# Attention, MLP and spectral mixing on one core: channel products of two row blocks side by side, the first theta phase keyed sooner, one threshold per couple of rows, new costs in the build's order

## The chip, the cores and the metric

The kernel runs on one core of a Trainium2 chip. The metric is the device time in microseconds, the median of three runs. TensorE (PE) multiplies; VectorE (DVE), ScalarE (ACT) and GpSimd (POOL) work on tiles; SyncE (SP) issues most DMAs. PE accumulates in eight PSUM banks.

## The reference

Four batches of 576 tokens, 512 wide (8 heads of 64). Three stages follow each other:

```python
scores = scale * np.matmul(q, k.transpose(0, 1, 3, 2))
thresh = np.max(scores, axis=-1, keepdims=True) - tau
scores = np.where(scores >= thresh, scores, -1000000000.0)
attn = np.exp(scores - max); attn = attn / (sum + 1e-09); x = attn @ v

xn = (x - mu) / np.sqrt(var + 1e-06) * g_ln
x = x + np.maximum(xn @ w_ch1, 0.0) @ w_ch2          # 512 -> 2048 -> 512

theta = x @ w_theta                                   # 512 -> 512
y = w_tok_r @ (x * cos(theta)) + w_tok_i @ (x * sin(theta))   # over tokens
u = x + y
out = u + np.maximum(u @ w_ch, 0.0)                   # 512 -> 512
```

(The second and third blocks are shortened to their formulas.)

## The kernel before, in words

**The order of the work.** The program writes no order by hand. Each piece of work is an `op` with the engines that may do it and a cost in ns on each, the ops it depends on, the buffers that it takes and gives back (`Slot` of a `Res`), a kind and, for PE, a key. `Plan.run` (L124) places them one by one as a list scheduler: on PE, among the ops that can start at the same moment, the one with the lowest key goes first; on the other engines the one with the lowest ready time plus the kind's offset (`OFF`, L71). An op with several possible engines goes where it ends first by its costs. Instructions are issued on each engine in this order, so a changed cost can change engine and place of anything behind it. Where PE would stand idle for over 200 ns, `keep` (L339) puts small filler matmuls (`warm`, L345); this ends with attention.

**Precision.** fp32 products are made of fp32r parts: an operand is split into a high part (`hi`) and a rest (`lo`), and three matmuls replace one.

**Attention** takes batch by batch in couples of two row tiles (`couple`, L691; `unit` for each row). `qk` (L720) gives S; `top` (L784, DVE) reads S, writes E = -S and the row's extreme `bt`; `thresh` (L791 on ACT, L793 elsewhere) adds tau to a 128x1 tile, `thr`; `mask` (L797) and the exponential (L800) follow on ACT; then E is split and turned by DMA, and `pv` (L748) multiplies by v. The first half of the MLP (eight chunks of the hidden width, part A: first product `p_A` L515, hidden part `h_A`, second product `chA` L538) runs between, one group of three row tiles at a time. `ln_group` (L885) makes a group's normalised rows: norm on ACT (L935), three transposes on PE (`ptr`, L944), then a copy out of PSUM (`flat`) and the `hi` and `lo` parts.

**PSUM.** Four banks (`rM`) serve all through, four belong to S in attention. `turn` (L1049) gives those four to the group `rC`.

**Part B** does the other eight hidden chunks (steps of 12 `p_B` and 9 `c` matmuls) for the six groups (1,2), (1,0), (1,1), (0,0), (0,1), (0,2), the first number being the pair of batches. `cvt` (L350) makes weights' two parts from the raw ones in eight ops (DVE L375 to L392, POOL, ACT): `tok` for the token mix, `cw` for the channel product.

**Spectral stage**, one batch b at a time: `transposes(b)` (`pt`, L1241) and `thetas(b)` (`th`, `th_t`, L1288; five tiles), `make_z(b)` (x cos, x sin and their parts: `z`), `mix(b)` (`y`, L1451: 54 matmuls for each of four blocks of 128 channels; sums `u` L1473 and L1478 take the two banks of a block and give them back; then `x1T` and `x1Tl`, the parts of u), `chan(b)` (`o`, L1508: 24 matmuls for each block, 6 for each of the four blocks of u that it sums over; `uo`, L1521 and L1526). The first phase's key is set by `T0STEP` (L67), in steps of the last group of part B. Each block of `chan` took two banks of `rM`, and `ylast[1]` made each block's first product depend on the block before:

```python
sl = [Slot(rM), Slot(rM)]
...
o = op(mm(kk), [o or ylast[1], d["c"][kk], cw_ops[kk]], sl if kk == 0 else (), T=6 * mm_(288),
       key=key + 0.01 * c)
```

## Time and profile before

| | before |
|---|---|
| median of 3 runs | 943.57 us (943.29 to 943.91) |
| the profiled execution's own time | 943.46 us |
| its span (first to last instruction) | 941.6 us |
| mean granted clock of PE, 1 being full speed | 0.978 |
| PE, DVE, ACT, POOL busy | 888.4, 677.7, 530.2, 537.7 us |
| DMA | 111.93 MB, 119 GB/s on the mean |

Everything that is said of durations comes from this one profiled execution. Busy times are sums over instructions on an engine; for PE they hold the pipelined ends of matmuls, so a busy PE need not be a PE at its peak. A wait is idle time of an engine ahead of an instruction, with the instruction that ended it.

### The profile page before, as it was taken

Reading aid. Unit: us, or ns where it says so; the run is one execution under the profiler, and the core shown is the slowest. Engines: PE = TensorE matmul, PEld = TensorE weight load, DVE = VectorE, ACT = ScalarE, POOL = GpSimd, SP = SyncE. Lnnn points to the kernel's source line nnn. Section 1 sums busy time; section 2 is a strip of 40 time slices with the busy share of each in tenths; the row PEclk is TensorE's granted clock in tenths of the full one; section 3 lists DMA queues with packets and bytes.
Section 4 is the critical chain, followed back from the end, with each engine's and each line's share of the span. In section 5 each row is a group of like instructions: output and inputs, shape, how many; then the busy total and the mean of one; then the engine's idle time right before and its main releaser. Section 6 shows DMA issues by size and latency. Waiting matters only on the chain. (4 is left out here: it accounts for less than half of the span.)

```text
span 941.6 us, 18946 instructions
## 1 busy us (share of the span) xinstructions
PE 888.4 (94%) x7287; PEld 789.3 (84%) x7287; DVE 677.7 (72%) x1227; ACT 530.2 (56%) x968; POOL 537.7 (57%) x614
## 2 busy tenths in 40 slices
PE   9787879999999999999999999999989899999998
PEld 7665668878888888888888899989977789899998
DVE  6899989788897887783788692221489873697734
ACT  7787778888887878883556561111356330453300
POOL 5999899779887887781556771000266530263400
PEclk9898899999999999999999999999999899999999
DMA  7889796799789988792555660340021111010011
GB/s 195 171 189 184 168 199 119 138 227 176 148 180 174 184 183 145 158 165 48 190 168 168 202 190 7 100 154 1 1 77 57 28 42 39 12 63 1 14 38 51
DMA packets 224954, 111.93 MB, mean 119 GB/s; under 512 B 174048, under 2 KB 206304, under 8 KB 224864
## 3 DMA queue, kind: packets, MB, share of 16 engines
q1 hardware_dynamic: 224576, 110.72, 51.6%
...
q10 hardware_dynamic: 288, 0.00, 0.0%
...
## 5 line engine op out<-in xcount | busy, mean ns | idle before, releaser
L229 POOL TENSOR_TENSOR P<-E,P 128x64 f16<-128x64 f32 (+1 forms) x194 | 144.4, 759 | 14.6 <-DVE P L224 5.8
L784 DVE TENSOR_SCALAR_CACHE_REDUCE E<-S 128x576 f32<-128x576 f32 x144 | 105.4, 747 | 25.6 <-PE S L720 16.3
L797 ACT ACTIVATE E<-E,thr 128x576 f32<-128x576 f32 x144 | 108.0, 768 | 11.5 <-POOL thr L793 10.1
L515 PE MATMUL p_A<-xt,w 128*128 128x384 f32 x576 | 112.9, 343 | 1.7 <-issue 1.5
L1451 PE MATMUL y<-tok,z 128*128 128x288 f32 x768 | 109.7, 301 | 4.9 <-DVE u L1473 3.7
L515 PE MATMUL p_B<-xt,w 128*128 128x384 f32 x576 | 111.1, 341 | 1.4 <-DVE w L414 1.4
L538 PE MATMUL c<-w,h_B 128*128 128x512 f32 x432 | 108.9, 395 | 3.6 <-DVE h_B L524 2.0
L538 PE MATMUL chA<-w,h_A 128*128 128x512 f32 x432 | 111.0, 400 | 1.4 <-DVE h_A L524 1.4
L1451 PEld LDWEIGHTS y<-tok,z 128*128 128x128 f32 x768 | 106.2, 193 | 5.9 <-DVE u L1473 4.2
L515 PEld LDWEIGHTS p_B<-xt,w 128*128 128x128 f32 x576 | 103.8, 190 | 6.3 <-DVE w L414 2.3
L800 ACT ACTIVATE E<-E,ntaup 128x576 f32<-128x576 f32 x144 | 107.5, 767 | 0.9
L720 PE MATMUL S<-khi,q 64*128 64x288 f32 (+1 forms) x576 | 85.9, 328 | 21.3 <-DVE E L784 18.3
L515 PEld LDWEIGHTS p_A<-xt,w 128*128 128x128 f32 x576 | 98.2, 188 | 5.6 <-issue 4.3
L538 PEld LDWEIGHTS c<-w,h_B 128*128 128x128 f32 x432 | 80.1, 188 | 19.5 <-DVE h_B L524 3.1
L538 PEld LDWEIGHTS chA<-w,h_A 128*128 128x128 f32 x432 | 78.0, 188 | 18.2 <-issue 2.1
L748 PEld LDWEIGHTS <-PT 128*128 128x128 f16 (+1 forms) x2240 | 75.9, 101 | 17.0 <-issue 14.5
L720 PEld LDWEIGHTS S<-khi,q 64*128 64x128 f32 (+1 forms) x576 | 56.8, 192 | 37.6 <-DVE E L784 23.1
L748 PE MATMUL pv<-va,PT 128*128 128x65 f16 (+1 forms) x2240 | 84.1, 195 | 3.4 <-DVE va L224 2.3
L521 ACT ACTIVATE h_B<-p_B 128x384 fp32r<-128x384 f32 x48 | 23.6, 491 | 110.8 <-PE p_B L515 110.8
L524 DVE SCALAR_TENSOR_TENSOR h_B<-p_B,h_B 128x384 fp32r<-128x384 f32 x48 | 26.6, 553 | 72.6 <-ACT h_B L521 72.3
L229 DVE TENSOR_TENSOR P<-E,P 128x512 f16<-128x512 f32 (+1 forms) x94 | 69.6, 759 | 4.9 <-POOL P L226 3.3
L226 POOL TENSOR_SCALAR P<-E 128x576 f16<-128x576 f32 x85 | 64.7, 764 | 14.3 <-ACT E L800 13.0
...
## 6 DMA issues: line engine op xcount, KB each, us to landing
...
```

Of the source, the lines that this page charges most:

```text
L226: G.tensor_scalar(out=out, in0=in_, scalar1=1.0, scalar2=0.0, op0=ALU.mult, op1=ALU.add)
L229: e.tensor_tensor(out=out, in0=a, in1=b, op=ALU.subtract)
L515: T.matmul(st["ps"][:, :n], lhsT=ch.w1(a, c), rhs=xt()[:, c, bb, :n], start=(kk == 0), stop=(kk == 11))
L521: A.activation(out=st["h"][:, 0, :n], in_=st["ps"][:, :n], func=AF.Relu)
L524: V.scalar_tensor_tensor(out=st["h"][:, 1, :n], in0=st["ps"][:, :n], scalar=0.0, in1=f(st["h"][:, 0, :n]), op0=ALU.max, op1=ALU.subtract)
L538: T.matmul(ps, lhsT=h[:, a, t * 128:(t + 1) * 128], rhs=ch.w2(bb), start=(first and (a, bb) == M2[0]), stop=(stop and (a, bb) == M2[2]))
L720: T.matmul(w["S"][:, n, 0:288], lhsT=qd.q["t"][r, a, hp], rhs=d.k[bb][r, n * 288:(n + 1) * 288], start=(k == 0), stop=(k == 2))
L748: T.matmul(out[:, j * 65:j * 65 + n], lhsT=l, rhs=r[:, j * 65:j * 65 + n], start=(k == 0), stop=(k == len(seq) - 1))
L784: V.tensor_scalar(out=st["e"].rearrange("p (a k) -> p a k", a=2), in0=st["S"][:, :, 0:288], scalar1=-1.0, scalar2=None, op0=ALU.mult, op1= ...
L797: A.activation(out=st["e"], in_=st["e"], func=AF.Prelu, bias=st["thr"], scale=-1.0, alpha=STEEP)
L800: A.activation(out=st["e"], in_=st["e"], func=AF.Exp, bias=ntaup, scale=1.0)
L1451: T.matmul(st["ps"][n][:, 0:288], lhsT=a, rhs=w[:, n * 288:(n + 1) * 288], start=(k == 0 and q == 0), stop=(k == 8 and q == 2))
```

## The change

- `T0STEP` is 1 instead of 5: PE's keys for the first transposes and thetas stand four steps sooner in the last group of part B.
- Many costs are others: `gc` (two-input operations on POOL) 2.5 instead of 2.11 ns a column, DVE operations with two inputs from SBUF 1.5 instead of 1.04 (`V2`), single-input copies 0.95 instead of 0.52, the conversion steps 1.1, 0.95 and 1.45, `top` 830 instead of 880 ns.
- The conversion of `w_ch` gets a kind of its own, `late`, whose offset in `OFF` is 25000 instead of 6000.
- The two rows of a couple share `bt` and `thr` (128x2), and one `thresh` follows both tops; the masks read their column of it. `taup2` holds tau twice.
- `chan`: every other block takes its two banks from `rC`, and the dependence of a block on the block before is gone.
- Code for an unused way of turning E is removed.

The diff, cut; left out are `taup2`'s setup, the entry in `OFF`, and further costs that change in the same way:

```diff
@@ -64,11 +64,14 @@
-T0STEP = 5
+T0STEP = 1
...
+LATE = 25000.0
+GC = 2.5
+V2 = 1.5
...
@@ -244,7 +247,7 @@
-        return 145.0 + 2.11 * n
+        return 145.0 + GC * n
@@ -418,9 +422,9 @@
         ob = op(s1b, [o], A=ac(n), **kw)
-        o = op(s2a, [oa], G=gc1(n), V=vc(n, .52), **kw)
-        o = op(s2b, [o], V=vc(n, .52), **kw)
-        o = op(s2c, [o], (), [sa], V=vc(n), **kw)
+        o = op(s2a, [oa], G=1550.0, V=vc(n, 1.1), **kw)
+        o = op(s2b, [o], V=vc(n, .95), **kw)
+        o = op(s2c, [o], (), [sa], V=vc(n, 1.45), **kw)
         o = op(s3, [o, ob], G=gc(n), **kw)
@@ -772,29 +776,34 @@
             scaled(tile_)
 
-    def unit(st, o_qk, d, whole, pen0, kw, cp, spv, sx_):
+    def unit(st, us, o_qk, d, whole, pen0, kw, cp, spv, sx_):
 
         nm, j = st["nm"], st["j"]
...
         def top(e):
 
-            st["bt"] = ap.tile([128, 1], F32, tag="bt", bufs=8, name="bt_" + nm)
+            if "bt" not in cp:
+                cp["bt"] = ap.tile([128, 2], F32, tag="bt", bufs=6, name="bt_" + nm)
+            st["bt"] = cp["bt"][:, j:j + 1]
             st["e"] = ap.tile([128, 576], F32, tag=str(es), name="E_" + nm)
             V.tensor_scalar(out=st["e"].rearrange("p (a k) -> p a k", a=2), in0=st["S"][:, :, 0:288], scalar1=-1.0,
...
         def thresh(e):
 
-            st["thr"] = ap.tile([128, 1], F32, tag="thr", bufs=8, name="thr_" + nm)
-            if e is A:
-                A.activation(out=st["thr"], in_=st["bt"], func=AF.Identity, bias=taup, scale=1.0)
+            m = len(us)
+            cp["thr"] = ap.tile([128, 2], F32, tag="thr", bufs=6, name="thr_" + nm)
+            if e is G:
+                G.tensor_tensor(out=cp["thr"][:, 0:m], in0=cp["bt"][:, 0:m], in1=taup2[:, 0:m], op=ALU.add)
+            elif e is A:
+                A.activation(out=cp["thr"][:, 0:m], in_=cp["bt"][:, 0:m], func=AF.Identity, bias=taup2[:, 0:1], scale=1.0)
             else:
-                e.tensor_tensor(out=st["thr"], in0=st["bt"], in1=taup, op=ALU.add)
+                V.tensor_scalar(out=cp["thr"][:, 0:m], in0=cp["bt"][:, 0:m], scalar1=taup2[:, 0:1], scalar2=None, op0=ALU.add)
 
         def mask(e):
 
-            A.activation(out=st["e"], in_=st["e"], func=AF.Prelu, bias=st["thr"], scale=-1.0, alpha=STEEP)
+            A.activation(out=st["e"], in_=st["e"], func=AF.Prelu, bias=cp["thr"][:, j:j + 1], scale=-1.0, alpha=STEEP)
 
         def expo(e):
@@ -813,36 +822,19 @@
...
+
+        st["rest"] = lambda o: rest_of(o, whole, pen0, kw, es, s16, spt, mask, expo, hi16, lo16, lo16t, tr)
+        st["top"] = op(top, [o_qk], (es,), (ss,), V=830, kind="top", **kw)
+        cp.setdefault("tops", []).append(st["top"])
+        if len(cp["tops"]) < len(us):
+            return None
+        o_thr = op(thresh, cp["tops"] + [k_tau], A=290, G=320, V=160, kind="thr", pen=pen0, **kw)
+        return [u["rest"](o_thr) for u in us]
+
+    def rest_of(o, whole, pen0, kw, es, s16, spt, mask, expo, hi16, lo16, lo16t, tr):
         o = op(mask, [o], A=EXP, kind="mask", **kw)
         o_mask = op(expo, [o], A=EXP, kind="exp", **kw)
-        if whole:
-            o = op(turn_p, [o_mask, k_pool] + turned[-1:], (stp,) + ((spv,) + sx_ if j == 0 else ()), (es,), T=640,
-                   kind="att", **kw)
-            turned.append(o)
-            o = op(take, [o], (spt,), (stp,), A=ac(512), V=690, kind="hi16", **kw)
-            return op(take_tail, [o], A=265, V=290, kind="hi16", **kw)
-        o = op(hi16, [o_mask], (s16,), A=ac(576), V=vc(576, .52), G=gc1(576), kind="hi16", pen=dict(pen0 or {}, A=HPA), **kw)
+        o = op(hi16, [o_mask], (s16,), A=ac(576), V=vc(576, .95), G=gc1(576), kind="hi16", pen=dict(pen0 or {}, A=HPA), **kw)
         es.uses = 2
         o1 = op(lo16t, [o], (), (es,), V=230, G=430, kind="lo16", **kw)
         o2 = op(lo16, [o], (), (es,), G=1210, V=LOV, kind="lo16", **kw)
@@ -1177,7 +1169,7 @@
-                    o_, sls if k == 0 else ())
+                    o_, sls if k == 0 else (), kind=kind)
@@ -1194,7 +1186,7 @@
     cw, _, cw_ops = split_weight("cw", [(c * 512, 512, wch[c * 128:(c + 1) * 128, :]) for c in range(KB)],
-                                 [load_of(o[-1]) for o in tok_ops])
+                                 [load_of(o[-1]) for o in tok_ops], "late")
     conv_done = [load_of(cw_ops[-1])]
@@ -1379,8 +1371,8 @@
-            o_s = op(mul("si"), [o_si, xf[p, xt]], (), xs2, V=vc(512), G=gc(512))
-            o_c = op(mul("co"), [o_co, xf[p, xt]], (), xs2, V=vc(512), G=gc(512))
+            o_s = op(mul("si"), [o_si, xf[p, xt]], (), xs2, V=vc(512, V2), G=gc(512))
+            o_c = op(mul("co"), [o_co, xf[p, xt]], (), xs2, V=vc(512, V2), G=gc(512))
@@ -1485,16 +1477,16 @@
-            sl = [Slot(rM), Slot(rM)]
+            sl = [Slot(rC), Slot(rC)] if c % 2 else [Slot(rM), Slot(rM)]
@@ -1511,10 +1503,10 @@
             o = None
             for kk in range(KB):
-                o = op(mm(kk), [o or ylast[1], d["c"][kk], cw_ops[kk]], sl if kk == 0 else (), T=6 * mm_(288),
+                o = op(mm(kk), [o, d["c"][kk], cw_ops[kk]], sl if kk == 0 else (), T=6 * mm_(288),
                        key=key + 0.01 * c)
 
-            ylast[1], o_pre = o, o.deps[0]
+            o_pre = o.deps[0]
 
             def pre(e, c=c, st=st, sn=sn):
@@ -1529,7 +1521,7 @@
-            o_p = op(pre, [o_pre, d["c"][c]], [sn], V=vc(576), G=gc(576), kind="ev")
+            o_p = op(pre, [o_pre, d["c"][c]], [sn], V=vc(576, V2), G=gc(576), kind="ev")
```

How instructions stand on the engines before and after, at three places. First PE at the end of attention, where the last products of part A (`chA_1_c_4`: block 1, row tile c) meet the transposes `ptr_2_t` of the next group's three tiles. Before:

```order
L538 MATMUL chA_1_1_4_7979<-w_4_0_1783,h_A_1_5_7915 128x512 x3
L944 MATMUL ptr_2_0_7992<-ident,xn_2_0_7983 128x128 x4
L538 MATMUL chA_1_1_4_7979<-w_4_1_2426,h_A_1_6_7946 128x512 x3
L944 MATMUL ptr_2_1_8001<-ident,xn_2_1_7989 128x128 x4
L538 MATMUL chA_1_1_4_7979<-w_4_1_2426,h_A_1_7_7965 128x512 x3
L538 MATMUL chA_1_2_4_8012<-w_4_0_1783,h_A_1_4_7867 128x512 x3
L538 MATMUL chA_1_2_4_8012<-w_4_0_1783,h_A_1_5_7915 128x512 x3
L538 MATMUL chA_1_2_4_8012<-w_4_1_2426,h_A_1_6_7946 128x512 x3
L538 MATMUL chA_1_2_4_8012<-w_4_1_2426,h_A_1_7_7965 128x512 x3
L944 MATMUL ptr_2_2_8033<-ident,xn_2_2_8023 128x128 x4
L515 MATMUL p_A_2_0_8048<-xt_2_8009,w_0_0_594 128x384 x2
```

And after:

```order
L542 MATMUL chA_1_2_4_7858<-w_4_0_1848,h_A_1_4_7701 128x512 x3
L542 MATMUL chA_1_2_4_7858<-w_4_0_1848,h_A_1_5_7744 128x512 x3
L542 MATMUL chA_1_2_4_7858<-w_4_1_2533,h_A_1_6_7765 128x512 x3
L542 MATMUL chA_1_2_4_7858<-w_4_1_2533,h_A_1_7_7811 128x512 x3
L936 MATMUL ptr_2_0_7880<-ident,xn_2_0_7876 128x128 x4
L936 MATMUL ptr_2_1_7889<-ident,xn_2_1_7885 128x128 x4
L936 MATMUL ptr_2_2_7909<-ident,xn_2_2_7901 128x128 x4
L519 MATMUL p_A_2_0_7925<-xt_2_7894,w_0_0_519 128x384 x2
```

The first two transposes moved from between the products to behind the last one, beside the third, with `p_A_2_0`, which reads all three, right behind.

Second DVE around the last two hidden parts of part B, `h_B_2_6` and `h_B_2_7` (`a_cw`, `raw_cw`: steps of the conversion of `w_ch`; `t`, `r`, `co`, `z`: `make_z(0)` and theta evictions). Before:

```order
L1374 TENSOR_TENSOR co_0_10007<-xl_0_9408,co_0_10007 128x512
L387 TENSOR_SCALAR a_cw_10025<-a_cw_10025 128x512
L392 SCALAR_TENSOR_TENSOR raw_cw_9971<-raw_cw_9971,a_cw_10025 128x512
L375 TENSOR_SCALAR a_cw_10054<-raw_cw_10014 128x512
L383 TENSOR_SCALAR a_cw_10054<-a_cw_10054 128x512
L387 TENSOR_SCALAR a_cw_10054<-a_cw_10054 128x512
L524 SCALAR_TENSOR_TENSOR h_B_2_6_10068<-p_B_2_6_9992,h_B_2_6_10068 128x384
L392 SCALAR_TENSOR_TENSOR raw_cw_10014<-raw_cw_10014,a_cw_10054 128x512
L1298 TENSOR_SCALAR t_0_2_10093<-t_0_2_10093 128x512
L1374 TENSOR_TENSOR r_0_9978<-xl_1_9414,r_0_9978 128x512
L1307 SCALAR_TENSOR_TENSOR r_2_10117<-t_0_2_10093,th_2_10003 128x512
L524 SCALAR_TENSOR_TENSOR h_B_2_7_10111<-p_B_2_7_10078,h_B_2_7_10111 128x384
```

And after:

```order
L232 TENSOR_TENSOR z_2_9921<-r_2_9718,z_2_9921 128x512
L528 SCALAR_TENSOR_TENSOR h_B_2_6_9939<-p_B_2_6_9917,h_B_2_6_9939 128x384
L232 TENSOR_TENSOR z_2_9921<-co_2_9854,z_2_9921 128x512
L232 TENSOR_TENSOR z_3_9956<-r_2_9718,z_3_9956 128x512
L387 TENSOR_SCALAR a_tok_9961<-a_tok_9961 128x432
L391 TENSOR_SCALAR a_tok_9961<-a_tok_9961 128x432
L528 SCALAR_TENSOR_TENSOR h_B_2_7_9982<-p_B_2_7_9952,h_B_2_7_9982 128x384
L396 SCALAR_TENSOR_TENSOR raw_tok_9891<-raw_tok_9891,a_tok_9961 128x432
```

The steps for `w_ch` are no longer there; the theta evictions and most of `make_z(0)` lie ahead of this place, and two steps for `tok` stand in it.

Third PE at the channel products of batch 0, with all numbers in the names: `o_0_c_n` is block c, half n, of batch 0; `y_1_0_n` is the first block of the mix of batch 1. Before:

```order
L1508 MATMUL o_0_0_0_10614<-x1T0_9856,cw1_10083 128x288
L1508 MATMUL o_0_0_1_10615<-x1T0_9856,cw1_10083 128x288
L1451 MATMUL y_1_0_0_10645<-tok00_8925,z_1_0_10563 128x288
L1451 MATMUL y_1_0_1_10646<-tok00_8925,z_1_0_10563 128x288
L1451 MATMUL y_1_0_0_10645<-tok01_8937,z_1_0_10563 128x288
L1451 MATMUL y_1_0_1_10646<-tok01_8937,z_1_0_10563 128x288
```

And after:

```order
L1500 MATMUL o_0_0_0_10458<-x1T0_9605,cw1_10249 128x288
L1500 MATMUL o_0_0_1_10459<-x1T0_9605,cw1_10249 128x288
L1500 MATMUL o_0_1_0_10488<-x1T0_9605,cw0_10234 128x288
L1500 MATMUL o_0_1_1_10489<-x1T0_9605,cw0_10234 128x288
L1500 MATMUL o_0_1_0_10488<-x1T0_9605,cw0_10234 128x288
L1500 MATMUL o_0_1_1_10489<-x1T0_9605,cw0_10234 128x288
```

Behind the first 18 products of block 0 there came 24 of the next mix, then the other 6, then blocks 1 to 3 with 24 each. Now 18 products each of blocks 0, 1 and 2 and 12 of block 3 come first, then the 6 or 12 left of each, and the next mix behind them all.

## Rows read from the trace of the kernel before

**Rows 1.** The page, busy time of each engine, its share of the span, instructions

```profile
PE 888.4 (94%) x7287; PEld 789.3 (84%) x7287; DVE 677.7 (72%) x1227; ACT 530.2 (56%) x968; POOL 537.7 (57%) x614
```

**Rows 2.** Stretches: us; PE, PEld, DVE, ACT, POOL busy; clock, DMA share, GB/s

```profile
0.00:132.70 132.70, 107.14 (x1129) 89.00 (x1129) 115.54 (x212) 100.13 (x178) 114.48 (x141) 0.90 0.84 179
211.30:451.00 239.70, 236.45 (x2554) 204.63 (x2554) 188.02 (x418) 183.56 (x339) 179.43 (x259) 1.00 0.83 157
451.00:530.00 79.00, 75.48 (x367) 67.40 (x368) 67.33 (x107) 45.47 (x96) 51.61 (x39) 0.98 0.55 174
530.00:702.00 172.00, 171.15 (x862) 154.07 (x860) 77.02 (x110) 55.33 (x99) 48.76 (x41) 1.00 0.26 85
746.00:786.80 40.80, 38.58 (x257) 38.35 (x258) 25.44 (x37) 11.96 (x20) 12.94 (x8) 0.89 0.17 56
```

**Rows 3.** The same view of the stretch that ends with the second `u` sum

```profile
704.70:745.90 41.20, 34.29 (x195) 29.11 (x193) 37.75 (x53) 23.10 (x40) 24.55 (x18) 0.99 0.17 50
```

**Rows 4.** Instruction groups: count, busy us, mean ns, idle before and its releasers

```profile
L784 DVE TENSOR_SCALAR_CACHE_REDUCE E<-S 128x576 f32<-128x576 f32 x144 | 105.4, 747 | 25.6 <-PE S L720 16.3 <-POOL P L229 6.8 <-ACT E L800 1.1
...
L793 POOL TENSOR_TENSOR thr<-bt,taup 128x1 f32<-128x1 f32 x70 | 22.6, 324 | 28.9 <-DVE E L784 17.6 <-DVE vsc L616 10.2 <-DVE den L861 0.5
```

**Rows 5.** PE in order of time: start, us, engine, line, operation, count, [idle before]

```profile
129.84 2.89 PE L345 MATMUL warm<-one 128*128 128x256 bf16 x25
```

**Rows 6.** PE in order of time, the end of attention

```profile
450.98 8.58 PE L515 MATMUL p_A<-xt,w 128*128 128x384 f32 x48 [1.45 <-issue]
```

**Rows 7.** ACT in order of time, just before it

```profile
449.63 0.60 ACT L222 ACTIVATE xn<-ptr 128x512 f32<-128x512 f32 x1 [2.18 <-PE ptr L944]
450.25 0.63 ACT L222 ACTIVATE xt<-xn 128x512 fp32r<-128x512 f32 x1
```

**Rows 8.** PE in order of time, the stretch of weight conversion

```profile
481.86 4.19 PE L538 MATMUL chA<-w,h_A 128*128 128x512 f32 x17 [1.40 <-DVE h_A L524]
...
513.79 2.71 PE L538 MATMUL c<-w,h_B 128*128 128x512 f32 x9 [0.58 <-ACT h_B L521]
...
517.85 0.45 PE L515 MATMUL p_B<-xt,w 128*128 128x384 f32 x1 [0.65 <-DVE w L414]
```

**Rows 9.** PE in order of time, from the last group to the second `u`

```profile
702.79 2.11 PE L538 MATMUL c<-w,h_B 128*128 128x512 f32 x8 [1.64 <-DVE h_B L524]
...
743.95 0.40 PE L1451 MATMUL y<-tok,z 128*128 128x288 f32 x1 [2.09 <-DVE u L1473]
745.97 9.04 PE L1451 MATMUL y<-tok,z 128*128 128x288 f32 x47 [1.61 <-DVE u L1473]
```

**Rows 10.** DVE in order of time, same stretch, and one row of later

```profile
700.88 1.38 DVE L387 TENSOR_SCALAR a_cw<-a_cw 128x512 uint32<-128x512 uint32 x1
702.19 0.55 DVE L524 SCALAR_TENSOR_TENSOR h_B<-p_B,h_B 128x384 fp32r<-128x384 f32 x1
...
707.71 1.80 DVE L229 TENSOR_TENSOR z<-r,z 128x512 fp32r<-128x512 f32 x1
...
758.12 0.69 DVE L229 TENSOR_TENSOR z<-r,z 128x512 fp32r<-128x512 f32 x1 [0.79 <-ACT z L222]
```

**Rows 11.** POOL in order of time, beside the third of these

```profile
707.19 1.77 POOL L229 TENSOR_TENSOR cw<-raw_cw,cw 128x512 fp32r<-128x512 f32 x1
```

**Rows 12.** PE in order of time, mixes and channel products

```profile
755.65 6.56 PE L1451 MATMUL y<-tok,z 128*128 128x288 f32 x48
...
762.85 2.57 PE L1508 MATMUL o<-x1T,cw 128*128 128x288 f32 x18
...
771.10 11.88 PE L1508 MATMUL o<-x1T,cw 128*128 128x288 f32 x76 [2.22 <-DVE x1T L229]
...
830.85 0.40 PE L1508 MATMUL o<-x1T,cw 128*128 128x288 f32 x1 [0.94 <-DVE uo L1526]
...
888.38 10.38 PE L1508 MATMUL o<-x1T,cw 128*128 128x288 f32 x76 [1.19 <-DVE x1T L229]
```

More of the change, by code (lines that the diff above doesn't have):

```diff
@@ L66 @@
 NU = 1
-T0STEP = 5
+T0STEP = 1
 IDLE = 200.0
 BUSY = 0.7
+LATE = 25000.0
+GC = 2.5
+V2 = 1.5
 PEN = {"V": 1000.0, "A": 500.0, "G": 500.0}
-OFF = {"ln": -20000.0, "lnev": -10000.0, "cvt1": 0.0, "top": -500.0, "mask": -500.0, "exp": -5000.0, "thr": -2500.0, "hi16": 500.0, "lo16": -1500.0, "evict": -4000.0, "guard": -3000.0, "att": -1500.0, "prep": 0.0, "ev": -2500.0, "fill": -3000.0, "cvt": 6000.0}
+OFF = {"ln": -20000.0, "lnev": -10000.0, "cvt1": 0.0, "top": -500.0, "mask": -500.0, "exp": -5000.0, "thr": -2500.0, "hi16": 500.0, "lo16": -1500.0, "evict": -4000.0, "guard": -3000.0, "att": -1500.0, "prep": 0.0, "ev": -2500.0, "fill": -3000.0, "cvt": 6000.0, "late": LATE}
 class Res:
@@ L321, in c_tau @@
         V.tensor_scalar(out=coef, in0=taub, scalar1=0.0, scalar2=0.125, op0=ALU.is_ge, op1=ALU.mult)
-        V.tensor_scalar(out=taup, in0=taub, scalar1=0.0, scalar2=TAU_MAX, op0=ALU.max, op1=ALU.min)
-        V.tensor_scalar(out=ntaup, in0=taup, scalar1=-1.0, scalar2=None, op0=ALU.mult)
+        for k in range(2):
+            V.tensor_scalar(out=taup2[:, k:k + 1], in0=taub, scalar1=0.0, scalar2=TAU_MAX, op0=ALU.max, op1=ALU.min)
+        V.tensor_scalar(out=ntaup, in0=taup2[:, 0:1], scalar1=-1.0, scalar2=None, op0=ALU.mult)
     k_ones = op(c_ones, G=100, kind="att")
@@ L876, in scaled @@
         o = op(recip, [o], V=190, kind="guard")
[L877 removed]
+        x_ops[tile_] = [op(scale, [o], V=vc(512, V2), G=gc(512), kind="guard", pen={"G": G0} if p == 0 and t < 4 else None)]
     chunks, last_tr, hold = [], [], []
@@ L964, in spill @@
                 Q.dma_start(scr[p, gi][:, t], st["xf", t])
-            o = first = op(norm, [o_rs, first] + last_tr, (sn,), A=808, V=vc(512, .52), kind="ln")
+            o = first = op(norm, [o_rs, first] + last_tr, (sn,), A=808, V=vc(512, .95), kind="ln")
             if (p, gi) != (1, 2):
@@ L1165, in tile_kernel, with split_weight @@
     flush(pend.pop(), key + 1.5)
-    def split_weight(name, src_list, start):
+    def split_weight(name, src_list, start, kind="cvt"):
         sls = (Slot(rW), Slot(rW))
```

61 lines of the change are left out of this document (22 added, 39 removed).

## The prediction

> **What bounds the kernel now.** The page comes first: PE is busy for 888.4 of 941.6 us, and the other engines for 56 to 72% [rows 1]. That is an average, so the busy time by stretch is read next [rows 2]. It shows three different limits.
>
> Up to 132.70 us PE holds 107.14 us, DVE 115.54 and POOL 114.48: three engines share attention, and much of PE's part is filler (the `warm` matmuls, 25 in 2.89 us, so 0.116 us each [rows 5]), which the build puts where it expects PE to idle. From 211.30 to 451.00 us PE is at 236.45 of 239.70, from 530 to 702 at 171.15 of 172.00: there nothing is to be won, and added PE work costs its full length. Between these, at 451 to 530 and from 702 on, PE waits again, and those waits are the reserve.
>
> I then went through PE's order of time for its waits and what released them. At the end of attention one wait of 1.45 us [rows 6]. In the stretch of weight conversion, PE waits 1.40 us for `h_A`, 0.58 for `h_B` and 0.65 for a converted weight [rows 8]. In the last MLP group and the spectral stage it waits 1.64 us for `h_B`, then 2.09 and 1.61 for the two sums `u` that give the PSUM banks back [rows 9], and 2.22, 0.94 and 1.19 us around the channel products [rows 12]. The 41.20 us before those `u` waits end hold 34.29 us of PE and 37.75 of DVE [rows 3]: there DVE, at 92%, is the bound.
>
> **The change, step by step.** Times are set against the profiled 943.46 us (span 941.6 and 1.9 around it); the median of the runs shown, 943.57, is 0.1 above, so the forecast serves for both.
>
> *Joint threshold.* 144 small additions become 80. By the order POOL's fall from 70 to 33. At 0.324 us each (22.6 us for 70 [rows 4]) that frees 37 x 0.324 = 12.0 us of POOL, about half of it, 6.0, ahead of 211 us, where (up to 132.70 us) POOL is busy for 86% of the time and DVE for 87% [rows 2]. No one engine is the bound there, so I take half: **-3.0 us**, bounds -6 to +6. The upper bound is a price of the same edit: the first mask of a couple now waits for the second row's `top`, 0.747 us on DVE [rows 4]; of the 64 couples (80 additions are 64 for couples and 16 for rows alone) about 32 run ahead of 211 us, and eight of them, fully exposed, make 6.0. For the most part DVE works through both tops without a break between them, and ACT has the other couples' masks and exponentials to do, so I take the exposure as covered.
>
> *More filler.* Behind the first hidden-layer product of the second MLP group, in the stretch where PE is at 99%, the order has 46 fillers instead of 33: 13 x 0.116 = 1.5, of which I take **+1.4 us** (0 to 1.5; they cost nothing if PE truly waits there).
>
> *End of attention.* Before, two of three transposes of the next group stand between channel products, and only the third lies open: ACT's two copies behind it, 0.60 and 0.63 us [rows 7], make most of the 1.45 us wait [rows 6]. After, all three stand together behind the last product. Three times 1.23 is 3.7, and with the 0.2 us of handing over that the 1.45 holds besides, 3.9 us: **+2.5 us**. Bounds 0 (another engine takes copies) to 5 (the copies also queue behind a norm).
>
> *Conversion stretch, 451 to 530 us.* The conversion steps' new costs shift work between DVE, ACT and POOL, and the last weight is ready sooner relative to PE, which comes later by the step before. The three waits are 1.40 + 0.58 + 0.65 = 2.63 [rows 8]; I take **-2.5 us**. Bounds -5 (PE is busy for 75.48 of 79.00, and its clock is at 0.98 [rows 2]: 3.5 and 1.6 us) and +2.5 (dearer steps put the same waits elsewhere).
>
> *First theta phase sooner.* PE's theta products of batch 0 move from the last four steps of the last group to its first ones. They are the same products; the risk is a wait for an operand in a stretch where PE has none. Nothing shows it, so it lies between 0 and the 1.64 us of the nearest wait of the kind [rows 9], rounded up to 2: **+0.7 us**.
>
> *End of the last group to the `u` sums.* This is the largest term. Before, DVE does late `w_ch` conversions ahead of the MLP's `h_B` (1.38 us for one of their steps, straight ahead of an `h_B` of 0.55 [rows 10]) and, in the stretch, 53 operations of 0.712 us (37.75 us [rows 3] over its count). The order after has 42 in the same part of the program, the conversions (kind "late") behind it: 42 x 0.712 = 29.9 us, and at DVE's 92% 32.6 us. PE's work there falls too, by the 12 products of the theta tail, 2.9 us, which go to the stretch before where PE is full: 34.29 - 2.9 = 31.4. So the stretch lasts 32.6 and 2.9 are paid earlier: 35.5, against 41.20 + the 1.64 us wait just ahead [rows 9] = 42.84. That is **-7.4 us**; bounds -8.5 (PE alone: 31.4 + 2.9) and -3 (DVE keeps its queue and only the 1.64 and part of the `u` waits go).
>
> *Channel products of batch 0.* Before, PE has 18 of a block's 24 products and then 24 of the next mix until the last block `x1T` of the mix is there: they start at 762.85 and the wait ends at 771.10, so the chain behind the mix takes 8.25 us, 2.22 of it open [rows 12]. After, 18 + 18 + 18 + 12 = 66 channel products stand ahead of the first that needs that block. At 10.38 us for 76 [rows 12] they last 66 x 0.137 = 9.0 us, and the chain is covered with 0.8 to spare. Around it the granted clock of the stretch is 0.89, the lowest of those read behind the start [rows 2]: 47 mix products take 9.04 us behind the `u` waits where 48 take 6.56 later (2.6 us [rows 9, 12]), and 76 channel products 11.88 behind the 2.22 us wait against 10.38 in the third batch (1.5 us). Wait and clock together are 2.22 + 2.6 + 1.5 = 6.3. The first part of the clock's loss follows waits of which one may stay, so I take **-4.9 us**, bounds -6.3 and -2.
>
> *The later batches.* Their waits of 0.94 and 1.19 us [rows 12] go by the same two edits (banks of both groups; blocks side by side): 2.13, taken as **-2.0 us**, bounds -3 and -0.5.
>
> Unchanged in effect: removed dead code, `taup2` (one more tiny DVE operation at the start).
>
> Sum: -3.0 + 1.4 + 2.5 - 2.5 + 0.7 - 7.4 - 4.9 - 2.0 = -15.2, so 943.46 - 15.2 = **928.3 us**.
>
> **The rivals.** *DVE stays the bound before the `u` sums.* For it: its share of 92% [rows 3], and that conversions have to be done somewhere before the channel products. Then that term is -3, the channel term -2 (the clock stays down) and the conversion term 0: 928.3 + 4.4 + 2.9 + 2.5 = 938.1 us.
>
> *The joint threshold starves the masks (the other side).* Up to 211 us ACT and DVE feed each other in a chain of tops, masks and exponentials; if that chain is the true bound there, each exposed couple costs 0.747 us [rows 4]. Without the edit's gain the rest gives 931.3. From (943.5 - 931.3) / 0.747 = 16 couples on the whole gain is gone; with 24 of 32 exposed it is 931.3 + 17.9 = 949.2 us. For it: DVE is busy for 115.54 of 132.70 and ACT's order is nearly fixed by it. Against it: fillers show that PE has slack there, and there are several couples in flight.
>
> *POOL's added work slows DVE.* After the change POOL has some 10 more operations in the stretch of the channel products. A subtraction of z tiles on DVE takes 1.80 us beside a POOL subtraction of 1.77 us [rows 10, 11], and 0.69 at another time [rows 10]. Ten such delays of 1.11 are 11.1 us; with DVE's 25.44 of 40.80 [rows 2] it has 36.5 to do where PE, without its 6.3 us of losses, has 34.5. The stretch then ends 2.0 us later and the cover of the channel products is thin: 928.3 + 2.0 + 2.2 = 932.5 us. The Trainium skill states this as a rule (SBUF — State Buffer, section "SBUF: two separate sides"): VectorE with two SBUF inputs and a GpSimd operation that reads SBUF exclude each other for a whole instruction. The pair of rows agrees with it. By the rule, with every added POOL operation in DVE's way, the time is this rival's; by the rows in which DVE runs undisturbed it is the forecast's.
>
> *Only numbers change places:* each wait that goes comes back elsewhere, 943.5 us.
>
> **How the numbers follow.** Forecast 0.57, DVE stays the bound 0.18, POOL slows DVE 0.08, starved masks 0.12, no change 0.05. About 0.2% (1.9 us) is what a measurement of this kernel can tell from nothing. The first three are all faster, 0.83; no change 0.05 and a share of the starved masks near the break-even 0.01 are the same, 0.06; the rest, 0.11, is slower. Around 928.3 the bounds of the single terms, which don't all fall on one side, make about 921 to 936. To leave out no more than 2 in 10 the range also takes in the DVE rival with its own error: 921 to 942.
>
> **What the changed profile would show.** Right: 8 us less between the last `h_B` and the second mix block; channel products of batch 0 without a break over 1 us, with the stretch's clock near 1.00; three transposes in a row ahead of a wait of about 4 us at the end of attention; the first 211 us within 3 us of before. Wrong: waits on `u` of over 1 us that remain, DVE at over 95% before them; the stretch up to 211 us longer, with ACT waiting on `thr`; DVE operations of about 1.8 us in a row beside POOL's behind the first mix; a new wait on the theta products early in the last group.

## The result and the profile after

The changed kernel takes 922.62 us (median of 4 runs, 921.74 to 923.57) against 943.43 (also 4 runs, 943.24 to 943.91): a ratio of 0.978, 95% interval 0.976 to 0.980, so 20.8 us or 2.2% less. The forecast was 928.3 with a range of 921 to 942. The profiled execution took 923.36 us with a span of 921.6; the span before was 941.6, so the traces have 20.0 us to explain.

The page of the changed kernel, busy time by engine, answers to [rows 1]:

```profile
PE 884.3 (96%) x7340; PEld 790.6 (86%) x7340; DVE 678.3 (74%) x1226; ACT 532.1 (58%) x958; POOL 515.2 (56%) x562
```

PE is the fuller engine by share only because the span is shorter. The stretches show where. The busy time by stretch of the changed kernel (columns as in [rows 2]): last group to first channel product, the last 42 us of that, and channel products of batch 0 to the second mix block of batch 1:

```profile
652.60:745.64 93.04, 93.04 (x539) 84.72 (x537) 70.15 (x107) 48.28 (x84) 36.90 (x29) 1.00 0.19 57
704.00:745.60 41.60, 41.60 (x279) 39.29 (x278) 39.99 (x59) 21.84 (x37) 24.84 (x20) 1.00 0.23 68
745.64:771.74 26.10, 22.73 (x168) 21.85 (x167) 23.77 (x27) 13.06 (x23) 19.20 (x12) 1.00 0.27 87
```

The kernel before, the same view, from its last group to its first channel product, which is the same PE work (539 records in both):

```profile
656.21:762.85 106.64, 98.03 (x539) 87.32 (x537) 78.66 (x111) 50.74 (x90) 50.65 (x38) 0.97 0.13 38
```

This stretch cut at the start of the third mix block, and the second part of it in the changed kernel:

```profile
656.21:743.95 87.74, 80.74 (x430) 70.25 (x428) 65.68 (x92) 43.70 (x78) 43.79 (x34) 1.00 0.13 40
743.95:762.85 18.90, 17.28 (x109) 17.07 (x109) 12.98 (x20) 7.04 (x13) 6.87 (x5) 0.82 0.09 29
731.24:745.64 14.40, 14.40 (x111) 14.40 (x109) 13.64 (x18) 7.85 (x13) 9.33 (x8) 1.00 0.22 72
```

106.64 us have become 93.04, all of them PE time at a granted clock of 1.00, the upper of its two levels, 2.4 GHz. Of the 13.6 us that went, 8.6 were idle (106.64 - 98.03) and 5.0 were PE time (98.03 against 93.04). Of these 5.0, 2.9 lie from the third mix block on, where the clock was at 0.82 (17.28 against 14.40). The other 2.1 lie ahead of it (80.74 against 93.04 - 14.40), at a clock of 1.00; there waits cut PE's work into more pieces, each with an end that counts as busy, which fits but was not taken apart.

PE in order of time in the changed kernel, the rows that answer to [rows 6], [rows 8], [rows 9] and [rows 12]:

```profile
447.44 1.11 PE L936 MATMUL ptr<-ident,xn 128*128 128x128 f32 x4 [2.89 <-ACT xn L927]
450.00 10.41 PE L519 MATMUL p_A<-xt,w 128*128 128x384 f32 x48 [1.45 <-POOL xt L229]
...
513.28 0.50 PE L542 MATMUL c<-w,h_B 128*128 128x512 f32 x1 [0.58 <-ACT h_B L525]
514.59 2.12 PE L542 MATMUL c<-w,h_B 128*128 128x512 f32 x8 [0.81 <-DVE h_B L528]
...
731.24 6.56 PE L1443 MATMUL y<-tok,z 128*128 128x288 f32 x48
...
745.64 9.23 PE L1500 MATMUL o<-x1T,cw 128*128 128x288 f32 x68
755.04 0.53 PE L1500 MATMUL o<-x1T,cw 128*128 128x288 f32 x2 [0.17 <-POOL x1T L232]
756.80 3.73 PE L1500 MATMUL o<-x1T,cw 128*128 128x288 f32 x26 [1.23 <-POOL cw L232]
762.50 5.29 PE L1443 MATMUL y<-tok,z 128*128 128x288 f32 x36 [1.97 <-DVE uo L1518]
...
869.78 6.38 PE L1500 MATMUL o<-x1T,cw 128*128 128x288 f32 x46 [1.32 <-DVE x1T L232]
```

From the last group on the waits for `h_B`, `z` and `u` are gone: the third mix block starts at 731.24 without one. In the channel products of batch 0 the 2.22 us wait is gone too, but 0.17 + 1.23 + 1.97 = 3.37 us of others stand there: for the last block's parts, for the converted `w_ch`, and for the sums `uo` that give the banks back.

### The profile page after: what moved, and what is told of

Its sections match the earlier page's. It is cut to its first block, busy times and chain, and to the rows that moved or that the text cites. A ratio compares the mean times of both kernels' runs of the same rounds, so it can differ in the third digit from the quotient of the medians.

```text
span 921.6 us, 19019 instructions
## 1 busy us (share of the span) xinstructions
PE 884.3 (96%) x7340; PEld 790.6 (86%) x7340; DVE 678.3 (74%) x1226; ACT 532.1 (58%) x958; POOL 515.2 (56%) x562
## 4 chain that ended last, share of the span: by engine, by line
PE 74%; DVE 8%; POOL 3%; issue 3%; ACT 1%; DMA 0%; DVEq 0%; POOLq 0%; ACTq 0%; SPq 0%
PE p_A L519 11%; PE chA L542 11%; PE p_B L519 11%; PE c L542 10%; PE y L1443 9%; PE S L724 6%; PE pv L752 6%; PE th L1280 4%; PE o L1500 3%; DVE z L232 1%; PE pt L1233 1%; PE warm L349 1%; PE ptr L936 1%; DVE P L232 1%; PE th_t L1280 1%
## 5 line engine op out<-in xcount | busy, mean ns | idle before, releaser
L232 POOL TENSOR_TENSOR P<-E,P 128x64 f16<-128x64 f32 (+1 forms) x174 | 136.4, 803 | 5.3 <-ACT P L225 2.1
L806 ACT ACTIVATE E<-E,thr 128x576 f32<-128x576 f32 x144 | 105.1, 767 | 8.1 <-POOL thr L798 7.0
L519 PE MATMUL p_B<-xt,w 128*128 128x384 f32 x576 | 108.7, 337 | 0.1
L1443 PE MATMUL y<-tok,z 128*128 128x288 f32 x768 | 106.5, 296 | 2.0 <-DVE uo L1518 2.0
L1443 PEld LDWEIGHTS y<-tok,z 128*128 128x128 f32 x768 | 103.6, 189 | 2.6 <-DVE uo L1518 2.4
L519 PEld LDWEIGHTS p_A<-xt,w 128*128 128x128 f32 x576 | 100.3, 191 | 5.1 <-issue 2.5
L809 ACT ACTIVATE E<-E,ntaup 128x576 f32<-128x576 f32 x144 | 104.4, 764 | 0.0
L724 PE MATMUL S<-khi,q 64*128 64x288 f32 (+1 forms) x576 | 83.5, 324 | 18.1 <-DVE E L790 18.0
L229 POOL TENSOR_SCALAR P<-E 128x576 f16<-128x576 f32 x96 | 72.2, 758 | 40.2 <-ACT E L809 37.0
L232 DVE TENSOR_TENSOR P<-E,P 128x512 f16<-128x512 f32 (+1 forms) x114 | 90.6, 814 | 2.6 <-POOL P L229 1.9
```

The lines of the kernel that those rows point to most:

```text
L229: G.tensor_scalar(out=out, in0=in_, scalar1=1.0, scalar2=0.0, op0=ALU.mult, op1=ALU.add)
L232: e.tensor_tensor(out=out, in0=a, in1=b, op=ALU.subtract)
L519: T.matmul(st["ps"][:, :n], lhsT=ch.w1(a, c), rhs=xt()[:, c, bb, :n], start=(kk == 0), stop=(kk == 11))
L724: T.matmul(w["S"][:, n, 0:288], lhsT=qd.q["t"][r, a, hp], rhs=d.k[bb][r, n * 288:(n + 1) * 288], start=(k == 0), stop=(k == 2))
L806: A.activation(out=st["e"], in_=st["e"], func=AF.Prelu, bias=cp["thr"][:, j:j + 1], scale=-1.0, alpha=STEEP)
L809: A.activation(out=st["e"], in_=st["e"], func=AF.Exp, bias=ntaup, scale=1.0)
```

## The experiments

Each was timed beside the kernel before on the same chip; the kernel before took 942.0 to 943.5 us there. Times in the text are medians, ratios come with their 95% intervals. In the table the spans are of one profiled execution each. It lies within 1.5 us of its kernel's median, but for "only costs" (2.9 us below) and "`w_ch` steps left out" (2.7 above); "last group" is the start of the 481st of the 576 `p_B` matmuls in PE's order of time, interpolated in its row, and the next columns run from there to the first `o`, and from that to the span's end.

| kernel | ratio to before | last group at | to first `o` | to the end | span |
|---|---|---|---|---|---|
| before | 1 | 656.2 | 106.6 | 178.8 | 941.6 |
| changed | 0.978 (0.976 to 0.980) | 652.6 | 93.0 | 176.0 | 921.6 |
| only T0STEP | 0.9965 (0.9953 to 0.9977) | 655.3 | 97.4 | 183.7 | 936.4 |
| only channel edit | 0.9968 (0.9956 to 0.9981) | 656.0 | 106.6 | 175.2 | 937.8 |
| only costs | 1.0029 (1.0014 to 1.0044) | 650.0 | 112.0 | 177.5 | 939.5 |
| only joint threshold | 1.0045 (1.0029 to 1.0061) | 659.3 | 106.2 | 179.1 | 944.6 |
| changed without T0STEP | 0.9953 (0.9937 to 0.9970) | 650.4 | 111.8 | 172.8 | 935.0 |
| changed without channel edit | 0.9842 (0.9822 to 0.9861) | 651.1 | 93.0 | 182.4 | 926.5 |
| changed without costs | 0.9938 (0.9922 to 0.9954) | 660.7 | 96.9 | 178.4 | 936.0 |
| changed without joint threshold | 0.9811 (0.9792 to 0.9830) | 652.6 | 93.0 | 177.4 | 923.0 |
| before, `w_ch` steps left out | 0.9960 (0.9945 to 0.9976) | 657.4 | 101.1 | 180.7 | 939.1 |
| T0STEP and costs only | 0.9872 (0.9848 to 0.9897) | 650.7 | 93.0 | 182.7 | 926.4 |
| changed, sums on DVE alone | 0.9775 (0.9750 to 0.9799) | 651.0 | 93.0 | 175.6 | 919.6 |
| changed, sums and z on DVE alone | 0.9782 (0.9757 to 0.9807) | 651.5 | 93.0 | 176.9 | 921.4 |

How far one such number can be read: the changed kernel and the four with the same instructions up to the last group reach it at 650.4 to 652.6, so 2 us there are scatter. From there to the first channel product, programs with the same order agree to 0.5 us (106.2 to 106.6; 97.4 and 96.9); where PE has no wait, all six come to 93.0.

The edit `late` needs no run. With its offset at 6000, as before, the changed kernel has the same instructions in the same order on every engine; the kernel before has them too with `late` alone added. It does nothing.

**One part alone.** T0STEP:

```diff
-T0STEP = 5
+T0STEP = 1
```

> The kernel before with T0STEP = 1 alone. Theory A (the theta phase keyed sooner frees DVE's queue of theta evictions and, with them, of conversions of w_ch ahead of the hidden parts and the u sums): the stretch from the last group to the third mix block gets 8 to 13 us shorter, 943.4 falls to 931 to 935 us. Rival B (the new costs reorder DVE there, the key does little): within 2 us of 943.4.

938.72 us, a time that neither theory gave. From the last group to the first channel product 9.2 us went (106.6 to 97.4), within theory A's 8 to 13; rival B falls in its form "the key does little". But behind that the kernel got 4.9 us longer, which no theory had. PE in order of time, this kernel:

```profile
719.78 0.54 PE L1435 MATMUL y<-tok,z 128*128 128x288 f32 x2 [1.62 <-ACT tok L225]
721.16 1.09 PE L1435 MATMUL y<-tok,z 128*128 128x288 f32 x3 [0.84 <-DVE tok L232]
...
761.47 0.50 PE L1492 MATMUL o<-x1T,cw 128*128 128x288 f32 x2 [3.29 <-DVE x1T L227]
763.24 12.90 PE L1492 MATMUL o<-x1T,cw 128*128 128x288 f32 x76 [1.26 <-POOL x1T L232]
```

The key does what it was meant to do for DVE's order: of the steps that convert `w_ch` on DVE, 8 of 13 stood ahead of the last hidden part, now none. What is left of the stretch above 93.0 is 1.62 + 0.84 us of waiting for the converted `tok`, and slower products behind it. The steps for `tok` are now pushed back by the sooner thetas: the last one ends 74.6 us behind the start of the last group, in the kernel before 35.2.

Behind the first channel product, the wait has grown from 2.22 [rows 12] to 3.29 + 1.26, and 76 products take 12.90 us instead of 11.88. DVE in order of time, just ahead of the `x1T` that the first of these waits ends with:

```profile
757.28 1.98 DVE L1505 TENSOR_TENSOR uo<-x1T 128x576 f32<-128x576 f32 x1
759.18 1.77 DVE L232 TENSOR_TENSOR z<-r,z 128x512 fp32r<-128x512 f32 x1
760.88 0.45 DVE L227 CAST x1T<-u 128x576 fp32r<-128x576 f32 x1
```

By the order 10 of the 13 `w_ch` steps now stand behind the first `u` sum of batch 0. That they are what makes `x1T` late is likely and not shown: right ahead of it stand a sum and a z tile.

The channel products:

```diff
-            sl = [Slot(rM), Slot(rM)]
+            sl = [Slot(rC), Slot(rC)] if c % 2 else [Slot(rM), Slot(rM)]
...
-                o = op(mm(kk), [o or ylast[1], d["c"][kk], cw_ops[kk]], sl if kk == 0 else (), T=6 * mm_(288),
+                o = op(mm(kk), [o, d["c"][kk], cw_ops[kk]], sl if kk == 0 else (), T=6 * mm_(288),
```

> The kernel before with the channel products' banks and dropped order alone. The prediction's terms (cover of the 2.22 us wait with the clock behind it, 0.94 and 1.19 us later): 943.4 falls by 4 to 6 us, to 938. Rival: as in the changed kernel's trace, where the channel products of batch 0 last as long as before with other waits, only the later waits go: -2 us, 941.

939.21 us, -3.0 by the ratio; 3.8 in the trace, 3.6 of it behind the first channel product. That lies between the two, in time nearer the rival, but not by its place: 2.2 us are won in batch 0. From the first channel product to the second mix block of batch 1 it takes 21.8 us (762.62 to 784.43) instead of 24.0 (762.85 to 786.82). PE in order of time, this kernel:

```profile
771.00 6.40 PE L1492 MATMUL o<-x1T,cw 128*128 128x288 f32 x46 [1.55 <-DVE x1T L232]
```

The wait for `x1T` is shorter, 1.55 instead of 2.22, and not covered.

The costs (the changed numbers of the plan, all of them):

```diff
-        return 145.0 + 2.11 * n
+        return 145.0 + GC * n
...
-        o = op(s2c, [o], (), [sa], V=vc(n), **kw)
+        o = op(s2c, [o], (), [sa], V=vc(n, 1.45), **kw)
```

> The kernel before with the new costs alone. Theory A: the conversion stretch loses 2 to 3 us of waits and the rest stays: 940 to 941 us. Rival B: the new costs are what reorders DVE before the u sums: 928 to 934 us.

944.21 us (12 runs, 941.3 to 950.0), slower by 0.3%: both wrong. The trace is of the fastest run. In it the costs win 6 us ahead of the last group (650.0 against 656.2) and lose 5.4 in the stretch behind it. They win ahead of the first `p_B` (479.6 against 485.9), not in the conversion stretch. PE in order of time, this kernel:

```profile
700.25 1.09 PE L1435 MATMUL y<-tok,z 128*128 128x288 f32 x3 [5.84 <-DVE z L227]
...
737.32 1.09 PE L1435 MATMUL y<-tok,zt 128*128 128x288 f32 x3 [5.29 <-ACT zt L225]
```

With the first phase at its old key the last group ends sooner, and then PE stands before z tiles that are not there, 5.84 and 5.29 us, with a clock of 0.92 over the stretch.

The joint threshold:

```diff
-        o = op(thresh, [o_top, k_tau], A=280, G=300, V=140, kind="thr", pen=pen0, **kw)
+        cp.setdefault("tops", []).append(st["top"])
+        if len(cp["tops"]) < len(us):
+            return None
+        o_thr = op(thresh, cp["tops"] + [k_tau], A=290, G=320, V=160, kind="thr", pen=pen0, **kw)
```

(with the costs of before.)

> The kernel before with one threshold per couple alone. Prediction: POOL and ACT freed, -3 us up to 211 us and nothing behind: 940.5 us. Rival (the second top is exposed): 2 us or more slower than 943.4.

946.09 us, 0.45% slower: the rival. The view of waits up to 480 us (engine and what waited, for what; us, times, longest), this kernel:

```profile
PE S L724 <- DVE E L790: 24.8, 27, 2.7
POOL P L229 <- ACT E L809: 27.1, 21, 3.2
```

and the kernel before:

```profile
PE S L720 <- DVE E L784: 18.3, 16, 3.4
POOL P L226 <- ACT E L800: 13.0, 13, 2.4
```

PE waits 6.5 us more for `top` to give S's banks back, POOL 14 us more for the exponentials. That fits masks that wait for the second `top`, but doesn't show it: ACT's own waits for `top` or `thr` add up to 31.1 us in this view, against 29.5 before.

**The change without one part.** Each undoes one of the four edits above.

> The changed kernel with T0STEP = 5 again. Theory A: the waits for h_B and u before the third mix block come back, 8 to 13 us slower than the changed kernel's 922.6: 931 to 935 us. Rival B (the new costs carry that gain): 922 to 926 us.

937.93 us. Theory A's side, and beyond its 935: the stretch is 111.8 instead of 93.0. Its order is that of the changed kernel up to the last group, so the 18.8 us are the key's alone. The waits are for z tiles, as with the costs alone, not for `h_B` and `u`.

> The changed kernel with the channel products in one bank group and in their old order. By the prediction's terms 4 to 7 us slower, 927 to 929 us. Rival (in batch 0 the new order only trades its wait for waits on the converted w_ch and on uo): 2 us slower, 925.

926.92 us. The edit is worth 6.4 us behind the first channel product (182.4 against 176.0), where the prediction's terms have 4.3. PE in order of time, this kernel:

```profile
749.01 0.89 PE L1443 MATMUL y<-tok,z 128*128 128x288 f32 x4 [2.33 <-ACT z L225]
752.17 1.09 PE L1443 MATMUL y<-tok,z 128*128 128x288 f32 x3 [2.27 <-DVE z L232]
```

Without the 66 channel products side by side PE goes on with the next mix, whose z tiles are late: 4.6 us in two waits.

> The changed kernel with the old costs. Theory A: 2 to 4 us of waits in the conversion stretch come back: 925 to 927 us. Rival B: over 8 us slower.

936.58 us, 14 more than the change: rival B. 8.1 us stand ahead of the last group, 3.9 in the stretch to the first channel product and 2.4 behind.

> The changed kernel with a threshold for each row again. Prediction: 3 us slower, 925.6 us. Rival (its gain in the start is nothing): within 1 us of 922.6.

924.84 us, ratio 0.9811 against 0.9779, intervals that overlap; the last group starts at 652.6 in both. In time nothing can be told apart. PE in order of time, this kernel, shows why:

```profile
445.00 0.66 PE L928 MATMUL ptr<-ident,xn 128*128 128x128 f32 x4 [0.46 <-ACT xn L919]
448.02 8.56 PE L519 MATMUL p_A<-xt,w 128*128 128x384 f32 x48 [2.37 <-issue]
...
504.67 1.14 PE L519 MATMUL p_B<-xt,w 128*128 128x384 f32 x5 [0.87 <-DVE w L418]
```

With a threshold for each row the three transposes do not stand together, and PE waits 0.46 + 2.37 us there instead of 2.89 + 1.45. On the other hand the wait for a converted weight, gone in the changed kernel, is there. All runs agree on this. The table has the start of the first `p_B` (us from the span's start) and, behind the semicolon, the time from there to the last group:

| | costs of before | new costs |
|---|---|---|
| threshold for each row | 485.7 to 487.0; 168.9 to 170.3 | 479.6 to 481.2; 170.4 to 171.4 |
| joint threshold | 490.4 and 490.7; 170.3 and 168.6 | 482.8 to 485.0; 167.6 |

So beside the new costs the joint threshold loses about 3 us ahead of the first `p_B` and wins about 3 behind it.

**What held DVE up.** In the kernel before, for pieces named `cw`, four of the steps return at once:

```diff
         def s2b(e):
+            if name[:2] == "cw":
+                return
```

> The kernel before, with four of the eight steps in the conversion of w_ch left out for each of its four pieces (the absolute value, the maximum, the shift and the joining of the words: 12 instructions on DVE, 2 on ACT, 2 on POOL), so that w_ch has wrong values; every other instruction stands in the same order. Theory A1 (the conversions of w_ch in DVE's queue are what holds the hidden parts and the u sums up): the waits of 1.64, 2.09 and 1.61 us go with the clock's loss behind them, the stretch from the last group to the first channel product falls from 109.4 to about 100 us, and the time to 933 to 935 us. Rival A2 (the late theta evictions and z tiles hold DVE, the conversions fill gaps): the stretch stays above 106 us, the time at 940 or more.

938.23 us, between the two, nearer the rival's time. The stretch falls by 5.5 us, from 106.6 to 101.1 (the 109.4 expected from, and the 95.7 of the next run, count from a mark 2.7 us sooner). A1 had 9.4 and A2 at most 3.4: neither. PE in order of time, this kernel, beside [rows 9] and [rows 12]:

```profile
740.53 0.40 PE L1459 MATMUL y<-tok,z 128*128 128x288 f32 x1 [0.22 <-DVE u L1481]
742.55 8.03 PE L1459 MATMUL y<-tok,z 128*128 128x288 f32 x47 [1.61 <-DVE u L1481]
...
767.43 3.97 PE L1516 MATMUL o<-x1T,cw 128*128 128x288 f32 x15 [2.98 <-DVE x1T L229]
```

DVE in order of time, this kernel, from behind the first of these two `u` sums to the second:

```profile
740.40 1.39 DVE L1382 TENSOR_TENSOR co<-xl,co 128x512 f32<-128x512 f32 x1
741.71 0.41 DVE L1321 TENSOR_SCALAR r<-r 128x512 f32<-128x512 f32 x1
742.05 0.44 DVE L1481 TENSOR_TENSOR u<-y,x1T 128x288 f32<-128x288 f32 x1
```

The conversions are behind the wait for `h_B_2_6` (1.64, none now) and the first for `u` (2.09, now 0.22). The waits for the hidden part after it stay, 0.30 + 0.96 us, where the kernel before has 0.92 + 0.34. The second wait for `u` stays at 1.61: a product of `make_z` and a theta eviction fill it. The run wins 5.5 us in this stretch where the sooner key wins 9.2; as it takes work away that the key only moves, it does not say how the 9.2 divide. And about a third of the gain is given back behind the first channel product (a wait of 2.98 instead of 2.22, 180.7 instead of 178.8 to the end).

**Two edits together.** The costs and T0STEP as above, nothing else.

> The kernel before with T0STEP = 1 and the new costs together, without the joint threshold and the channel products' edit. Theory A (these two only work together: sooner thetas empty DVE there, the costs place what is left): last group to first channel product 95.7 us, as in the changed kernel, and the channel stage 6 us longer than there: 927 to 930 us. Rival (the joint threshold has a share): over 932 us.

929.66 us: theory A, the stretch at its 93.0. Alone the two add up to nothing (-0.35% and +0.3%); together they are -1.3%. In this stretch PE waits for `tok` with the key alone and for z tiles with the costs alone; with both it waits for neither, and the last `tok` step ends 69.9 us behind the start of the last group instead of 74.6.

**POOL and DVE side by side.** In the changed kernel `post`, `lo_` and `pre` lose POOL as a choice:

```diff
-            o = op(post, [o, o1], V=vc(576, V2), G=gc(576))
+            o = op(post, [o, o1], V=vc(576, V2))
```

> The changed kernel with the sums behind the mix (the u of both halves, its rest x1Tl, the uo ahead of the channel product) on DVE alone instead of on DVE or POOL. Theory C (in the channel stretch DVE and POOL slow each other, DVE's operations taking 1.8 us instead of 0.7): the waits of 1.23 and 1.97 us there shrink and the time is 2 to 4 us below the changed kernel's, 919 to 921 us. Rival (DVE, at 96% in the 42 us before, has no room for them): the same or up to 4 us slower.

921.25 us; the ratio 0.9775 is the change's. The waits shrink from 3.37 to 2.07 us, all but 0.10 of it for the converted `w_ch`, but the clock over the 26 us from the first channel product on is 0.93 now instead of 1.00. In the changed kernel itself, DVE in order of time:

```profile
751.78 1.91 DVE L232 TENSOR_TENSOR z<-co,z 128x512 fp32r<-128x512 f32 x1
753.62 1.98 DVE L1513 TENSOR_TENSOR uo<-x1T 128x576 f32<-128x576 f32 x1
755.52 1.77 DVE L232 TENSOR_TENSOR z<-r,z 128x512 fp32r<-128x512 f32 x1
757.22 1.83 DVE L1513 TENSOR_TENSOR uo<-x1T 128x576 f32<-128x576 f32 x1
```

and POOL beside it:

```profile
753.10 1.89 POOL L232 TENSOR_TENSOR x1T<-u,x1T 128x576 fp32r<-128x576 f32 x1
754.94 1.80 POOL L232 TENSOR_TENSOR cw<-raw_cw,cw 128x512 fp32r<-128x512 f32 x1
```

These are the rows that the prediction named as the sign of its third rival. The next run takes the z tiles from POOL as well, in `make_z`:

```diff
-            o_s = op(mul("si"), [o_si, xf[p, xt]], (), xs2, V=vc(512, V2), G=gc(512))
+            o_s = op(mul("si"), [o_si, xf[p, xt]], (), xs2, V=vc(512, V2))
```

> The run before this one, with the products x cos and x sin and the rests of the z tiles on DVE alone too, so that POOL keeps only the steps of the weight conversions behind the last group. Theory C (the two engines in the same stretch cost each other more than POOL takes off): DVE's two-input operations take 0.7 us instead of 1.8 and the waits of the channel stretch go: 917 to 920 us. Rival (DVE gets more work than it wins): z tiles come late, new waits ahead of the mixes, 923 to 928 us.

923.06 us, again the same. A stretch of the channel products in this kernel, as long as the changed kernel's above (busy time, columns as in [rows 2]):

```profile
745.60:771.70 26.10, 24.01 (x168) 23.61 (x167) 19.89 (x37) 11.14 (x19) 1.37 (x1) 0.93 0.27 87
```

and PE in order of time there:

```profile
756.40 4.83 PE L1500 MATMUL o<-x1T,cw 128*128 128x288 f32 x22 [2.09 <-ACT cw L225]
```

The instruction groups of 700 to 765 us in the same kernel (count, busy us, mean ns, idle before):

```profile
L1513 DVE TENSOR_TENSOR uo<-x1T 128x576 f32<-128x576 f32 x4 | 3.0, 750 | 0.0
```

DVE does 37 operations in 19.89 us, 0.54 each, where it did 27 in 23.77, 0.88 each (all kinds together). Theory C is right about the engines and wrong about the time: the channel products now wait once, for the converted `w_ch`, 2.09 us, and behind that wait 22 of them take 4.83 us, where at full speed they need 22 x 0.137 = 3.0. From the first channel product to the mix behind the last it is 16.9 us in the changed kernel, 16.5 in the run before this one and 16.9 here. With the sums off POOL, what PE waits for is the conversion.

## Why the prediction was right, and where its terms were off

Direction and range held. By the table's three parts (up to the last group, from there to the first channel product, behind it) the forecast had -1.6, -9.3 and -4.3 us (the 2.6 us of clock behind the `u` waits counted with the middle part, where they stand); measured are -3.6, -13.6 and -2.8. The middle part, two thirds of the gain, was foreseen in kind. That the first part has the right sign is luck: its largest term, the joint threshold, points the wrong way, and what the costs win in attention stands in no term.

**Joint threshold, -3.0: wrong in sign.** Alone it is 0.45% slower. The waits of that run agree with the prediction's own opposite rival, masks that wait for the second top, without showing it; its size is smaller than the rival's 949 us. Beside the new costs its loss up to the first `p_B` comes back in the conversion stretch. What was won ahead of the last group comes from the costs: 650.0 to 652.6 in the runs that have them and not the threshold, 655.3 to 657.4 in those that have neither. Which of the many numbers does it was not tried.

**Fillers and the end of attention, +1.4 and +2.5.** The three transposes together cost PE 2.89 + 1.45 = 4.34 us of waiting where [rows 6] had 1.45: +2.9, as forecast. They stand together in every run with the joint threshold and in none without it, so this price is the threshold's too. Not foreseen was the clock behind it: the 48 `p_A` take 10.41 us instead of 8.58, at a granted clock of 0.81 instead of 1.00. That the fillers cost their length was not tested by itself.

**Conversion stretch, -2.5.** From the first `p_B` to the last group 170.3 us have become 167.6: -2.7. The wait of 0.65 for a weight is gone, and two shorter ones behind it; 0.58 for `h_B` stands as before, and 0.81 for the next one. (The 1.40, gone too, stands ahead of the first `p_B`, where the slower `p_A` use up what it gives: 34.9 us from the 48 `p_A` to there, 35.0 now.) The size is right; of its two reasons the first, the new costs, is not: with them and no joint threshold the stretch takes 170.4 to 171.4 us and PE still waits for the weight. The second, that PE comes later, fits: the weight's wait goes in the runs with the joint threshold.

**Thetas sooner and the way to the `u` sums, +0.7 and -7.4: right in mechanism, too small.** (42.84 - 35.5 makes -7.3.) The wait that +0.7 allows for did not come. The step that was mis-sized is "the stretch lasts 32.6", DVE's count at DVE's 92%. In the changed kernel, from `pt_1_0` to the third mix block:

```profile
701.97:731.24 29.27, 29.27 (x183) 26.68 (x181) 27.15 (x43) 15.43 (x27) 16.70 (x14) 1.00 0.22 63
```

DVE does 43 operations (42 were reckoned) at 93% (92%), but one takes 0.631 us on the mean and not 0.712, and PE has no wait in the 29.3 us: PE's work sets the time, not DVE. Later, in the 42 us up to the first channel product, DVE is at 96% and PE still never waits. A share of busy time says how full an engine is, not that it is late. Of the 4.3 us by which the middle part was missed, 3.3 are here; about 1.1 lie ahead of `pt_1_0`, where the stretch grew by 0.9 us and not by 0.7 + 2.9 - 1.64 = 2.0. The clock behind the `u` waits came out as reckoned, 2.5 us for 2.6 (745.90 to 762.85 before, 731.24 to 745.64 now). The 93.0 us are PE's own work there; six kernels reach them, and none with less than both T0STEP and the costs.

The credit was misplaced too. "The conversions (kind "late") behind it" names the wrong edit: the kind changes nothing, and it is the sooner thetas that put the conversions behind the hidden parts. Of DVE's `w_ch` steps none stands ahead of the last hidden part with the key alone, 3 of 12 with the costs alone, 8 of 13 before.

**Channel products, -4.9 and -2.0.** Of the wait of 2.22 us 0.17 is left (the chain behind the mix takes 9.4 us now, 745.64 to 755.04, not 8.25), but the step "the chain is covered" looked at `x1T` alone. What T0STEP moved out of the stretch before arrives here: `w_ch` is ready later (1.23 us), and the sums that free banks are late (1.97). PE in order of time, the changed kernel and then the kernel before:

```profile
767.62 1.91 PE L1233 MATMUL pt<-ident,xl 128*128 128x128 f32 x16
...
771.74 6.56 PE L1443 MATMUL y<-tok,z 128*128 128x288 f32 x48
...
786.82 6.56 PE L1451 MATMUL y<-tok,z 128*128 128x288 f32 x48
```

From the first channel product to this mix block it is 26.1 us (745.64 to 771.74), or 24.4 without the 1.7 of transposes that stood later before; the kernel before has 24.0 (762.85 to 786.82). So in batch 0 nothing is won behind the first channel product, where the terms have -2.3, and the later batches give about 3 for the 2.0 reckoned. T0STEP costs 4.9 to 5.2 us behind the first channel product (183.7 against 178.8, 182.7 against 177.5), 3.2 with the channel edit (176.0 against 172.8); the channel edit wins 5.3 to 6.4 there with the key and 3.6 to 4.7 without it. That its worth comes near its terms is partly luck: in the changed kernel it covers waits for z tiles (2.33 and 2.27 us without it), not the wait for `x1T` that the prediction reckoned with, and so pays a debt of the key.

**The rivals.** DVE as remaining bound is refuted (93.04 of 93.04 on PE). POOL slowing DVE is there; taking the work from POOL won nothing that the runs can tell. New costs without the key, or the key without them, are what the rivals should have held: each alone within 0.4% of before.
